# Five of six column blocks of a gMLP's input projection as matmuls of 64 rows, two token tiles at a time

## The chip, the cores and the metric

The kernel runs on one core of a Trainium2 chip. The metric is the device time of one execution in microseconds (us), given as the median of several runs. The engines are TensorE (PE, with weight loads, PEld, shown apart), VectorE (DVE), ScalarE (ACT), GpSimd (POOL) and SyncE (SP), which here only issues DMA transfers.

## The reference, cut to what matters

```python
def reference(A_x, A_wqkv, A_wo, B_x, B_w_in, B_w_sp, B_b_sp, B_w_out):
    # S = 2048 tokens, D = 576, 32 heads of 18, window 256, F = 4608, Fh = 2304
    xn = _layernorm(x)
    s = _A_ref(xn, A_wqkv, A_wo)          # causal sliding-window attention, then @ wo
    ...
    z = _gelu(xn @ w_in)                  # in _B_ref
    z1, z2 = z[..., :Fh], _layernorm(z[..., Fh:])
    g = einsum("ts,bsf->btf", w_sp, z2) + b_sp
    g = _silu((z1 * g) @ w_out)
    return x + s * g
```

The part that is changed is the right half of `xn @ w_in`, here called z2: 2048 tokens by 576 features times 576 by 2304.

## The kernel before, in words

All products are to be exact to about fp32. TensorE works on fp32r operands, so each factor is split into a high and a low part (`split`, L112 to L114: ACT copies the high part, DVE subtracts it from the source for the low one), and a product is three passes: high by high, low by high, high by low. The transposed, normalised input stays on chip as nine planes of 128 partitions: planes 0 to 3 hold the high parts of 512 features, planes 4 to 7 their low parts, and plane 8 the tail, 64 features with the high part on partitions 0 to 63 and the low part on 64 to 127. `norm_chunk` makes them for 512 tokens at a time: for the tail ACT copies the transposed tile (in which the 64 features stand twice), and DVE subtracts that copy from the source on the upper partitions (L290). The weights' tail stands twice as well, so two passes do for the tail, and `passes` (L221) yields 4 × 3 + 2 = 14 passes for an output tile.

The stages follow each other: input and norm with the q and k projections (`qk_chunk`), v, **z2**, attention with the z1 projection interleaved, wo, the products with w_sp, and the output. In a trace of before, z2 lies from 200.42 to about 441 us.

z2 is computed in six column blocks (`pc`) of 384 columns (ZW), each over 16 token tiles (`s`) of 128 tokens. For a tile, 14 matmuls (L720) accumulate in a PSUM bank `mm` (pool `mmp`, two buffers): the plane's 128 by 128 piece is the loaded operand, the weight's 128 by 384 piece the moving one. Then ACT evicts it with the gelu into half of a tile `zt` (L730; four buffers), DVE takes the statistics for z2's layernorm (L731), and after every second tile ACT issues the store of `zt` into `z2_d` in DRAM (L733). Three other strands run in the same loop:

- **Weights.** `load_z2(pc + 1)` (L673) fetches the next block's weights in three pieces of 128 columns: SP loads a piece into `z1wh` or `z1wl`, used here as raw buffers (L683), and ACT and DVE split it into `z2wh` and `z2wl`. It is a generator that is advanced at every second token tile. Block 0's weights were put in two of the attention's slots, `att0` and `att1`, and these are set to zeros and ones again (`clear`, L352 to L355, one by DVE and one by POOL) at the head of block 1.
- **Combinations of w_sp.** `sp_combos` (L642), a generator too, prepares sums of quadrants of w_sp for a later stage with fewer products: 16 steps, each with four SP loads (L651), four additions or subtractions on POOL (L661 to L665) and four SP stores into `sc_d` (L668), with two buffers of each kind. It is advanced at every second token tile.
- **Attention's operands.** From block 3 on, SP loads of the first heads (`pair_jobs`, L381); in block 5 the first row maxima (`row_max`, L428) lie between the passes.

The order on the engines: the gate, as this section is called, is within `order` (L671), which keeps the written order on PE, POOL and DVE (`ENGINES = {ET.PE, ET.Pool, ET.DVE}`, L55). The instructions of ACT and SP, and so all DMA issues, are put in order by a planner that simulates a timeline with its own costs (`schedule_with_timeline_sim=True`). From the attention on ACT and SP keep the written order too (L777). A tile's writers and readers wait for each other by semaphores that the framework inserts; completions of the DMAs are counted on eight semaphores that SP's and ACT's transfers share.

Of the kernel before, what the change touches and what calls it, by code (L numbers as in the profile page):

```python
# [9 lines left out]
F32 = mybir.dt.float32  # L10
F32R = mybir.dt.float32r
AF = mybir.ActivationFunctionType
ALU = mybir.AluOpType
PSUM = bass.MemoryType.PSUM
DRAM = bass.MemoryType.DRAM

P = 128
# [7 lines left out]
NS = S // P  # L25
# [3 lines left out]
ZW = 384  # L29
# [28 lines left out]
def f32(ap):  # L58
    return ap.bitcast(F32)
# [3 lines left out]
def kernel(  # L63
# [13 lines left out]
    act, dve, pool, pe, sp = nc.scalar, nc.vector, nc.gpsimd, nc.tensor, nc.sync  # L77

    def open_pool(stack, name, bufs=1, **kw):
        return stack.enter_context(tc.tile_pool(name=name, bufs=bufs, reuse_waits="tile", **kw))  # L80
# [9 lines left out]
    z2_d = dram.tile([S, FH], F32, name="z2_d")  # L90
# [14 lines left out]
    st2 = const.tile([P, NS, 6, 6], F32, name="st2")  # L105
# [21 lines left out]
    zt = []  # L127
# [57 lines left out]
    def plane(n, cs):  # L185

        i = 2 * n + cs.start // HS
        c0 = i % 3 * HS + cs.start % HS
        return xt6[i // 3][:, c0:c0 + cs.stop - cs.start]
# [6 lines left out]
    raws, halves, wpools = {}, {}, []  # L196
# [20 lines left out]
    with ExitStack() as early:  # L217
# [16 lines left out]
        with ExitStack() as ph:  # L234
# [23 lines left out]
            def norm_chunk(c):  # L258
                st = pA.tile([P, 4, 2, 6], F32, name="st")
                mv = pA.tile([P, 4, 2], F32, name="mv")  # L260
                sd = pA.tile([P, 4], F32, name="sd")
                rs = pA.tile([P, 4], F32, name="rs")
                tm = pA.tile([P, 4], F32, name="tm")
                step = 2 if c == 0 else 4
                for i0 in range(0, 4, step):
                    b = slice(i0, i0 + step)
                    for i in range(i0, i0 + step):
                        xr = xs[4 * c + i]
                        for j in range(2):
                            dve.bn_stats(st[:, i, j, :], xr[:, j * 288:(j + 1) * 288])  # L270
                        dve.bn_aggr(mv[:, i, :], st[:, i].rearrange("p a b -> p (a b)"))
                    rsqrt_of(rs[:, b], mv[:, b, 1], sd[:, b], tm[:, b])
                    for i in range(i0, i0 + step):
                        xr = xs[4 * c + i]
                        dve.tensor_scalar(xr[:, :D], xr[:, :D], mv[:, i, 0:1], rs[:, i:i + 1], ALU.subtract, ALU.mult)
                        pool.tensor_copy(xr[:, D:640], xr[:, 512:576])
                cs = slice(c * 512, (c + 1) * 512)
                for k in range(5):
                    t = tp.tile([P, 512], F32, name="tpt")
                    for i in range(4):  # L280
                        pe.transpose(t[:, i * P:(i + 1) * P], xs[4 * c + i][:, k * P:(k + 1) * P], ident)  # L281
                    if c == 0 and k < 2:
                        for i in range(3 + 3 * k):
                            pe.transpose(warm_up[:, k, i % 4 * P:(i % 4 + 1) * P], xs[3][:, :P], ident)
                    if k < 4:
                        split(plane(k, cs), plane(4 + k, cs), t)
                    else:
                        tail = plane(8, cs)
                        act.activation(tail, t, AF.Copy)
                        dve.tensor_tensor(tail[64:128], t[64:128], f32(tail[64:128]), ALU.subtract)  # L290

            def qk_chunk(c):
                cs = slice(c * 512, (c + 1) * 512)
# [54 lines left out]
        with ExitStack() as ph:  # L348
# [323 lines left out]
            with ExitStack() as gate:  # L672
                def load_z2(pc):  # L673
                    if pc:
                        wh, wl = (gz.tile([P, 5, ZW], F32R, name=n) for n in ("z2wh", "z2wl"))
                    else:
                        wh, wl = (slots[i][:, :5 * ZW].rearrange("p (k n) -> p k n", k=5) for i in range(2))

                    def pieces():
                        for c in range(3):  # L680
                            cs = slice(c * P, (c + 1) * P)
                            raw = f32(zw.tile([P, 5, P], F32R, name=("z1wh", "z1wl")[c % 2]))
                            sp.dma_start(raw, w_z2[:, :, pc * ZW + c * P:pc * ZW + (c + 1) * P])  # L683
                            yield
                            split(wh[:, :, cs], wl[:, :, cs], raw)
                            yield

                    return wh, wl, pieces()

                nxt = load_z2(0)  # L690
                for _ in nxt[2]:
                    pass
                for _ in vm:
                    pass
                values.close()
                gz = open_pool(gate, "gz", bufs=2)
                ahead = iter(())
                combos = sp_combos(gate)
                pairs = []
                for pc in range(6):  # L700
                    zc = slice(pc * ZW, (pc + 1) * ZW)
                    wh, wl, _ = nxt
                    if pc + 1 < 6:
                        nxt = load_z2(pc + 1)
                    if pc == 1:
                        clear(0)
                        clear(1)
                    if pc == 3:
                        pairs = [job for p in range(2) for job in [pair_jobs(p)] for _ in range(8)]
                    if pc == 5:  # L710
                        pairs = [job for job in [pair_jobs(2)] for _ in range(8)]
                        ahead = row_max(0)
                    for s in range(NS):
                        ss = slice(s * P, (s + 1) * P)
                        if pairs:
                            next(pairs.pop(0))
                        ps = mmp.tile([P, 512], F32, name="mm")
                        pl = list(passes(wh, wl, ss))
                        for n, (wt, r) in enumerate(pl):
                            pe.matmul(ps[:, :ZW], r, wt, start=n == 0, stop=n == len(pl) - 1)  # L720
                            if n in (3, 7, 11):
                                next(ahead, None)
                        if (pc * NS + s) % 2 == 1:
                            next(combos, None)
                        if pc + 1 < 6 and s % 2 == 0:
                            next(nxt[2], None)
                        if s % 2 == 0:
                            zz = gz.tile([P, 2 * ZW], F32, name="zt", bufs=4)
                        zv = zz[:, s % 2 * ZW:s % 2 * ZW + ZW]
                        act.activation(zv, ps[:, :ZW], AF.Gelu_apprx_tanh)  # L730
                        dve.bn_stats(st2[:, s, pc, :], zv)  # L731
                        if s % 2 == 1:
                            act.dma_start(z2_d[(s - 1) * P:(s + 1) * P, zc].rearrange("(a p) c -> p a c", p=P),  # L733
                                          zz.rearrange("p (a c) -> p a c", a=2))
                        if pc == 5 and s == 6:
                            z1_first.append(load_z1(0))
                        if pc == 5 and s == 12:
                            while z1_first[0][2]:
                                z1_first[0][2].pop(0)()
                        if pc == 5:  # L740
                            spend(0 if s < 12 else 1000)
                            dve.bn_aggr(mv2[:, s, :], st2[:, s].rearrange("p a b -> p (a b)"))
                for _ in ahead:
                    pass
                for _ in combos:
                    pass
                sd2 = gz.tile([P, NS], F32, name="sd2", bufs=1)
                tm2 = gz.tile([P, NS], F32, name="tm2", bufs=1)
                rsqrt_of(rstd2, mv2[:, :, 1], sd2, tm2)
                dve.tensor_tensor(nmr2, mv2[:, :, 0], rstd2, ALU.mult)  # L750
                dve.tensor_scalar(nmr2, nmr2, -1.0, None, ALU.mult)
# [23 lines left out]
            with ExitStack() as heads:  # L775
# [21 lines left out]
                for u in range(NU):  # L797
# [22 lines left out]
                    while due[0] or due[1] or filled < quota:  # L820
# [9 lines left out]
                        _, kind, n = due[pick[1]].pop(0)  # L830
# [6 lines left out]
                        s, j = items[n]  # L837
# [42 lines left out]
        with ExitStack() as ph:  # L880
# [39 lines left out]
            for n in range(NS):  # L920
                t, c = divmod(n, 2)
# [37 lines left out]
    with ExitStack() as ph:  # L959
# [180 lines left out]
        for m, (g, n, s) in enumerate(order_sp):  # L1140
            k = PRODUCTS[n][1]
# [3 lines left out]
            wh, wl, zh, zl = halves.pop(m)  # L1145
            for j in range(6):
                c, p = divmod(j, 3)
                cs, ps = slice(c * 512, c * 512 + 512), slice(p * P, p * P + P)
                for i, (z, w) in enumerate(((zh, wh), (zh, wl), (zl, wh))):
                    pe.matmul(acc[j], z[:, ps], w[:, cs], start=s == i == 0 and n in OPENS,  # L1150
                              stop=s == 7 and i == 2, skip_group_check=True)
# [34 lines left out]
    with ExitStack() as ph:  # L1186
# [25 lines left out]
        nxt = load_y(CH[0])  # L1212
# [92 lines left out]
```

## Time and profile before

| | us |
|---|---|
| median of the runs shown (3) | 1955.36 |
| lowest, highest | 1953.27, 1958.51 |
| span of the profiled execution | 1949.2 |
| PE busy in it | 1931.0 (99%) |
| DVE, ACT, POOL busy | 1050.1, 897.2, 283.5 |

| stretch of the profiled execution | from, to (us) |
|---|---|
| input, norm, q, k and v | 0 to 200.4 |
| z2, blocks 0 to 4 | 200.42 to 397.35 |
| z2, block 5, with the first row maxima | 397.35 to about 441 |

The span is that of the engines' instructions in one execution taken with the profiler; it stands a few us under the times of the runs. Busy time on PE is modelled from its instructions' starts, so a busy PE need not be PE at its best rate. The view by windows gives, for a stretch, the busy time and the number of instructions of each engine, the granted TensorE clock as a share of full speed, the busy share of the DMA engines, and what they moved.

### The profile page before, as it was taken

What the parts mean: (1) busy time and instruction counts of PE and PEld (TensorE: products, weight loads), DVE (VectorE), ACT (ScalarE), POOL (GpSimd) and SP (SyncE); (2) the same over time, 40 slices, a digit from 0 to 9 for tenths busy, and PEclk for the clock granted to TensorE, in tenths of its full rate; (3) what the DMA queues carried; (4) which work ended last, traced back from release to release, by engine and by line L of the source; (5) the groups of instructions that cost most, each with busy time, mean ns of one, the idle gap of its engine ahead of it and who ended that gap; (6) DMA issues with size and microseconds to landing.
All of it is one profiled execution on the core that took longest, in us unless ns stands there. A gap on an engine that the chain in (4) does not pass through costs nothing.

```text
span 1949.2 us, 30859 instructions
## 1 busy us (share of the span) xinstructions
PE 1931.0 (99%) x11159; PEld 1656.4 (85%) x11159; DVE 1050.1 (54%) x2294; ACT 897.2 (46%) x1674; POOL 283.5 (15%) x362
## 2 busy tenths in 40 slices
PE   8999999999999999999999999999999999999999
PEld 7889999997777777777698888888888888899998
DVE  5511233366666666665226787757876567663222
ACT  4222322215555556566557675555554534442111
POOL 5001366103222222323200000000000000000000
PEclk9999999999999999999999999999999999999999
DMA  8655799424554556564567777776677555875441
GB/s 266 175 149 157 256 352 349 168 80 137 143 160 135 164 142 160 138 149 127 179 226 253 251 234 249 230 234 214 200 245 240 185 174 186 266 235 160 140 143 58
DMA packets 221513, 375.60 MB, mean 193 GB/s; under 512 B 43312, under 2 KB 118448, under 8 KB 221232
## 3 DMA queue, kind: packets, MB, share of 16 engines
q1 hardware_dynamic: 206000, 349.66, 57.9%
q10 hardware_dynamic: 15360, 23.97, 3.3%
q8 instruction: 88, 1.44, 0.3%
q14 instruction: 65, 0.53, 0.1%
HBM read 260.45 MB, written 112.83 MB: 192 GB/s over the span
## 4 chain that ended last, share of the span: by engine, by line
PE 91%; DMA 3%; DVE 2%; issue 2%; ACT 1%; POOL 1%; SPq 0%; ACTq 0%; DVEq 0%; POOLq 0%
PE acc L1150 32%; PE mm L484 12%; PE po L1243 12%; PE mm L720 9%; PE mm L312 6%; PE sp L428 5%; PE tps L554 5%; PE ops L578 4%; PE vps L504 3%; PE wops L910 3%; DMA a<-in_w_sp_dram 1%; DVE spl L114 1%; DMA zr<-z_d 1%; DMA sc_d<-a 0%; PE tpt L281 0%
## 5 line engine op out<-in xcount | busy, mean ns | idle before, releaser
L1150 PE MATMUL acc<-spl,zh 128*128 128x512 f32 x1008 | 392.6, 389 | 1.1 <-DVE spl L114 0.8
L1150 PE MATMUL acc<-sph,zl 128*128 128x512 f32 x1008 | 392.2, 389 | 0.0
L1150 PE MATMUL acc<-sph,zh 128*128 128x512 f32 x1008 | 392.2, 389 | 0.0
L432 DVE CUSTOM_DVE_ANT_0 junk<-sp,band 128x384 bf16<-128x384 f32 (+1 forms) x512 | 269.6, 538 | 160.4 <-PE sp L428 153.0
L558 ACT ACTIVATE pt<-tps 128x384 f32<-128x384 f32 (+2 forms) x576 | 243.7, 437 | 178.5 <-PE tps L554 168.8
L484 PE MATMUL mm<-b,z1wh 128*128 128x512 f32 x648 | 230.3, 395 | 0.0
L1150 PEld LDWEIGHTS acc<-spl,zh 128*128 128x128 f32 x1008 | 189.2, 188 | 41.7 <-DVE spl L114 2.8
L1150 PEld LDWEIGHTS acc<-sph,zh 128*128 128x128 f32 x1008 | 189.2, 188 | 39.4
L1150 PEld LDWEIGHTS acc<-sph,zl 128*128 128x128 f32 x1008 | 189.2, 188 | 39.1
L114 DVE TENSOR_TENSOR spl<-spr,sph 128x1024 fp32r<-128x1024 f32 x168 | 205.2, 1221 | 30.7 <-ACT sph L113 28.4
L113 ACT ACTIVATE zh<-b 128x384 fp32r<-128x384 f32 x168 | 87.5, 521 | 230.4 <-PE acc L1150 230.3
L720 PE MATMUL mm<-z2wh,b 128*128 128x384 f32 x720 | 191.4, 335 | 1.8 <-ACT zt L730 1.8
L554 PE MATMUL tps<-att 128*128 128x384 f32 (+1 forms) x576 | 184.3, 326 | 0.8 <-ACT pt L558 0.7
L428 PE MATMUL sp<-att 128*128 128x384 f32 (+1 forms) x512 | 177.1, 350 | 1.1 <-DVE mx L432 0.8
L113 ACT ACTIVATE sph<-spr 128x1024 fp32r<-128x1024 f32 x168 | 175.9, 1047 | 1.6 <-DMA spr<-sc_d 1.4
L114 DVE TENSOR_TENSOR zl<-b,zh 128x384 fp32r<-128x384 f32 x168 | 92.9, 553 | 149.7 <-ACT zh L113 144.3
L1243 PE MATMUL po<-b,yh 128*128 128x288 f32 x840 | 147.1, 295 | 0.5 <-ACT gs L1230 0.5
L731 DVE BATCH_NORM_STATS2 st<-zt 128x6 f32<-128x384 f32 x96 | 53.5, 559 | 167.7 <-ACT zt L730 167.7
L484 PE MATMUL mm<-b,z1wl 128*128 128x512 f32 x360 | 142.0, 395 | 0.0
L428 PEld LDWEIGHTS sp<-att 128*128 128x128 f32 x512 | 95.3, 187 | 51.0 <-issue 25.7
L720 PE MATMUL mm<-z2wl,b 128*128 128x384 f32 x400 | 133.7, 334 | 0.0
L720 PEld LDWEIGHTS mm<-z2wh,b 128*128 128x128 f32 x720 | 130.4, 188 | 3.0 <-ACT zt L730 3.0
(187 smaller groups left out, 2872.7 us busy)
## 6 DMA issues: line engine op xcount, KB each, us to landing
spr<-sc_d SPq DMA_DIRECT2D x96, 512.0 KB
spr<-in_w_sp_dram SPq DMA_DIRECT2D x72, 512.0 KB
zr<-z_d SPq DMA_DIRECT2D x144, 192.0 KB
st_d<-qkhl SPq DMA_DIRECT2D x72, 256.0 KB
z_d<-zt ACTq DMA_DIRECT2D x48, 384.0 KB
z_d<-z1o SPq DMA_DIRECT2D x72, 256.0 KB
z1t<-z_d SPq DMA_DIRECT2D x72, 256.0 KB
y_d<-z1t SPq DMA_DIRECT2D x72, 256.0 KB
```

The source lines that it names most:

```text
L113: act.activation(hi, src, AF.Copy)
L114: dve.tensor_tensor(lo, src, f32(hi), ALU.subtract)
L312: pe.matmul(ps, w, r, start=n == 0, stop=n == len(pl) - 1)
L428: pe.matmul(ps[:, :w], q_of(u, j)[:, i * P:(i + 1) * P], k_of(u, j)[:, k0:k0 + w], start=True, stop=True)
L432: dve.tensor_tensor_reduce(out=junk[:, :w], in0=ps[:, :w], in1=band[:, m0:m0 + w], scale=1.0, scalar=-3.0e38, op0=ALU.add, op1=ALU.max, ac ...
L484: pe.matmul(ps, w, r, start=n == 0, stop=n == len(pl) - 1)
L554: pe.matmul(ps[:, :m * P], k_of(u, j)[:, (kb - base) * P:(kb - base + 1) * P], q_of(u, j)[:, (a - lo) * P:(a - lo + m) * P], start=True, s ...
L558: act.activation(pt[:, j, d0:d0 + n * P], ps[:, (qa - a) * P:(qa - a + n) * P], AF.Exp, scale=scale)
L578: pe.matmul(o_ps[c][32 * j:32 * j + 32, (lo - 4 * c) * P:(hi - 4 * c + 1) * P], vgs[u][:, kb - k0, j * VW:j * VW + 32], pt[:, j, (lo - kb) ...
L720: pe.matmul(ps[:, :ZW], r, wt, start=n == 0, stop=n == len(pl) - 1)
L1150: pe.matmul(acc[j], z[:, ps], w[:, cs], start=s == i == 0 and n in OPENS, stop=s == 7 and i == 2, skip_group_check=True)
L1243: pe.matmul(po[i][:, a, :288], y if ahead else y[:, i * P:(i + 1) * P], w[a], start=f == 0 and m == 0, stop=f == NF - 1 and m == 2)
```

## The change

In blocks 0 to 4 each pass over 128 partitions becomes two matmuls of 64 partitions, a **lower** one (partitions 0 to 63) and an **upper** one (64 to 127), both into the same PSUM tile. The tile is called `zmm`, from a new pool `zps` of three buffers; block 5 keeps the passes of 128 and `mm`. `z2_halves` makes the two lists. The tail takes three half matmuls instead of two full passes: high by high, low by high, and high by low; low by low is no longer computed. The third one goes to the lower half for tiles whose tail has its high part below, and to the upper half for the others. For that `norm_chunk` now stores the tail of every second 256 tokens with the parts exchanged, by two subtractions (lines 290 and 291 of the changed kernel) on 64 partitions and 256 columns each in place of one. So a tile has 14 lower and 13 upper halves or the reverse, and the tiles are taken in the order 0, 2, 1, 3 of each four, so that these kinds alternate.

The loop over a tile emits its lower halves (line 757 there), and behind each of them one upper half of an earlier tile (`z2_upper`, line 732 of the changed kernel), if there is one in the list `upper`. For the first two tiles of block 0 this begins only with the seventh lower half (`LAG = 6`), so that the upper halves keep that distance from then on. Behind the lower halves of a tile DVE copies two of its columns into `between` (line 761 there), a small tile that nobody reads; in the framework's order the copy reads the bank after the lower halves, and the upper halves write it after the copy. When a tile's last upper half is emitted, `z2_evict` does what the loop did before: gelu (line 724 there), statistics (725), and the store (728) once both tiles of a `zt` are there. At the end of block 4 the upper halves that are left are emitted, and block 5 runs as before. The weights, the combinations and the attention's loads are advanced at the same tiles as before, and the clears of `att0` and `att1` are written at the head of block 1 as before; the upper halves left from block 0's last tiles come behind them.

In the built program PE's instructions are the same as before in kind and order, other than the 2160 halves in place of 1120 passes. Lines of the changed kernel are one higher than before from L292 on, and 58 higher from L772 on.

```diff
@@ -287,7 +287,8 @@
                     else:
                         tail = plane(8, cs)
                         act.activation(tail, t, AF.Copy)
-                        dve.tensor_tensor(tail[64:128], t[64:128], f32(tail[64:128]), ALU.subtract)
+                        for r, a in ((slice(64, 128), slice(0, 256)), (slice(0, 64), slice(256, 512))):
+                            dve.tensor_tensor(tail[r, a], t[r, a], f32(tail[r, a]), ALU.subtract)
 
             def qk_chunk(c):
                 cs = slice(c * 512, (c + 1) * 512)
@@ -697,6 +698,42 @@
                 ahead = iter(())
                 combos = sp_combos(gate)
                 pairs = []
+                zps = open_pool(gate, "zps", bufs=3, space=PSUM)
+                zts, open_, upper = {}, [], []
+                LAG = 6
+
+                def z2_halves(wh, wl, s, ps):
+                    ss = slice(s * P, (s + 1) * P)
+                    odd = s // 2 % 2
+                    halves = []
+                    for up, r in enumerate((slice(0, 64), slice(64, 128))):
+                        ms = [m for k in range(4) for m in ((plane(k, ss)[r], wh[r, k]), (plane(k, ss)[r], wl[r, k]),
+                                                            (plane(4 + k, ss)[r], wh[r, k]))]
+                        ms.append((plane(8, ss)[r], wh[r, 4]))
+                        if up == odd:
+                            ms.append((plane(8, ss)[r], wl[r, 4]))
+                        halves.append([partial(pe.matmul, ps[:, :ZW], x_, w_, start=not up and n == 0,
+                                               stop=n == len(ms) - 1, skip_group_check=True) for n, (x_, w_) in enumerate(ms)])
+                    return halves
+
+                def z2_evict(pc, s, ps):
+                    if s // 2 not in zts:
+                        zts[s // 2] = gz.tile([P, 2 * ZW], F32, name="zt", bufs=4)
+                    zz = zts[s // 2]
+                    zv = zz[:, s % 2 * ZW:s % 2 * ZW + ZW]
+                    act.activation(zv, ps[:, :ZW], AF.Gelu_apprx_tanh)
+                    dve.bn_stats(st2[:, s, pc, :], zv)
+                    if s % 2 == 1:
+                        zz = zts.pop(s // 2)
+                        act.dma_start(z2_d[(s - 1) * P:(s + 1) * P, pc * ZW:(pc + 1) * ZW].rearrange(
+                            "(a p) c -> p a c", p=P), zz.rearrange("p (a c) -> p a c", a=2))
+
+                def z2_upper():
+                    upper.pop(0)()
+                    open_[0][1] -= 1
+                    if not open_[0][1]:
+                        z2_evict(*open_.pop(0)[0])
+
                 for pc in range(6):
                     zc = slice(pc * ZW, (pc + 1) * ZW)
                     wh, wl, _ = nxt
@@ -710,7 +747,28 @@
                     if pc == 5:
                         pairs = [job for job in [pair_jobs(2)] for _ in range(8)]
                         ahead = row_max(0)
-                    for s in range(NS):
+                    for i in range(NS if pc < 5 else 0):
+                        s = i // 4 * 4 + (0, 2, 1, 3)[i % 4]
+                        if pairs:
+                            next(pairs.pop(0))
+                        ps = zps.tile([P, 512], F32, name="zmm")
+                        lo, up = z2_halves(wh, wl, s, ps)
+                        for n, m in enumerate(lo):
+                            m()
+                            if upper and (pc or i > 1 or n >= LAG):
+                                z2_upper()
+                        between = gz.tile([P, 2], F32, name="between")
+                        dve.tensor_copy(between, ps[:, 0:2])
+                        upper += up
+                        open_.append([(pc, s, ps), len(up)])
+                        if i % 2 == 1:
+                            next(combos, None)
+                        if i % 2 == 0:
+                            next(nxt[2], None)
+                    if pc == 4:
+                        while upper:
+                            z2_upper()
+                    for s in range(NS if pc == 5 else 0):
                         ss = slice(s * P, (s + 1) * P)
                         if pairs:
                             next(pairs.pop(0))
```

## The prediction

> **What bounds the kernel now.** I read the page's busy shares and its chain first, then the stretches of the z2 stage by window, then the timeline of single engines there.
>
> ```profile
> span 1949.2 us, 30859 instructions
> PE 1931.0 (99%) x11159; PEld 1656.4 (85%) x11159; DVE 1050.1 (54%) x2294; ACT 897.2 (46%) x1674; POOL 283.5 (15%) x362
> PE 91%; DMA 3%; DVE 2%; issue 2%; ACT 1%; POOL 1%; SPq 0%; ACTq 0%; DVEq 0%; POOLq 0%
> 275.00:311.00 36.00, 36.00 (x209) 35.83 (x208) 10.99 (x18) 9.26 (x18) 22.41 (x18) 1.00 1.02 362
> 311.00:347.00 36.00, 36.00 (x209) 35.82 (x208) 11.44 (x19) 9.26 (x18) 21.84 (x17) 1.00 0.94 342
> ```
>
> TensorE sets the end nearly everywhere: it is busy for 99% of the span and holds 91% of the chain. The last two lines are two stretches of the z2 stage (columns: length, PE, weight loads, DVE, ACT, POOL, clock, DMA share, GB/s). PE is full in them, but so are the DMA engines, at 362 GB/s and a share of 1.02. Most of those bytes are the w_sp combinations, which only use this stage as cover: z2 does not need them. The timeline gives PE's pace:
>
> ```profile
> 200.42 38.99 PE L720 MATMUL mm<-att,b 128*128 128x384 f32 x224
> 239.25 0.51 PE L720 MATMUL mm<-z2wh,b 128*128 128x384 f32 x2
> 397.35 0.51 PE L720 MATMUL mm<-z2wh,b 128*128 128x384 f32 x2
> ```
>
> Block 0 takes 239.25 − 200.42 = 38.83 us, 173.3 ns for each of its 224 passes. Block 5, which the change leaves as it is, starts at 397.35. I work out where it starts afterwards; all that follows it has the same instructions and shifts with it.
>
> **The matmuls.** Before, a token tile takes 14 passes, 1120 over five blocks. After, the lower halves number 14 and 13 in turn, 1080 in all, and an upper half of the tile before goes beside each. Upper halves lag by six slots and a tile, so 20 of them are left over at the end and run alone. That makes 1100 slots, 20 fewer: −3.5 us at 173.3 ns, if a pair costs what a full pass costs. No row shows halves of rows side by side. The nearest shows four column tiles:
>
> ```profile
> 457.67 1.50 PE L578 MATMUL ops<-pt,vg 128*32 128x384 f32 x16
> L578 PE MATMUL ops<-pt,vg 128*32 128x384 f32 x512 | 47.9, 492 | 0.0
> 10.09 0.93 PE L281 MATMUL tpt<-ident,xr 128*128 128x128 f32 x7
> L281 PE MATMUL tpt<-ident,xr 128*128 128x128 f32 x80 | 11.2, 273 | 0.0
> 199.09 0.69 PE L504 MATMUL vps<-whv,b 128*128 128x288 f32 x4
> L504 PE MATMUL vps<-whv,b 128*128 128x288 f32 x288 | 53.0, 294 | 0.0
> L720 PEld LDWEIGHTS mm<-z2wh,b 128*128 128x128 f32 x720 | 130.4, 188 | 3.0 <-ACT zt L730 3.0
> ```
>
> Sixteen matmuls of 492 ns each begin within 1.50 − 0.49 us, 67 ns apart on the mean, each with a load of its own: disjoint tiles run together, loads included. Halves of rows share no partition either, so I take 173 ns for a pair. Lower bound: four matmuls of 288 columns start every (0.69 − 0.29)/3 = 132 ns, so 96 columns cost 41 ns and 384 cost 165; the remaining 8 ns could vanish beside the other half. Upper bound: the two loads of a pair share one path; load and transpose of 128 columns follow each other every (0.93 − 0.27)/6 = 110 ns, so a pair would take 220.
>
> The Trainium skill ("TensorE: Matmul & The Clock Gate", Measured speedup vs the span model) gives four row tiles 3.07 times the speed of one after another; as an estimate by that rate a slot is 173/0.77 = 226 ns, and the sum below would be some 37 us higher. Its rule under The mechanism, that a weight load overlaps a running matmul only in another row group, would make pairing hide loads that are paid for today. The trace disagrees with it: loads of 188 ns disappear in intervals of 173 ns, all in the same rows.
>
> **The small additions.** 80 copies of two columns (between) go to DVE. Nearest rows, from both sides:
>
> ```profile
> L432 DVE DVE_READ_ACCUMULATOR2_ANT mx<- 128x1 f32 x32 | 2.7, 83 | 0.0
> L742 DVE BATCH_NORM_AGGREGATE mv<-st 128x2 f32<-128x36 f32 x15 | 4.8, 317 | 0.5
> L731 DVE BATCH_NORM_STATS2 st<-zt 128x6 f32<-128x384 f32 x95 | 53.0, 559 | 166.2 <-ACT zt L730 166.2
> 239.47 1.81 POOL L354 MEMSET att<- 128x2048 f32 x1 [16.92 <-PE mm L720]
> 241.22 1.17 POOL L355 MEMSET att<- 128x1280 f32 x1
> ```
>
> That is 7 to 25 us on an engine busy for 11 of 36 us: work beside PE. But the copy is a wait too. A tile's first upper half needs it six slots (1.0 us) after its last lower half, and everything on PE is queued behind that half. A copy that stands behind one statistic of 0.56 us makes it; one behind a late weight split does not, and I count that with the transfers below. The tail's subtraction in two instructions instead of one lies in the start and beside other work: nothing. The clears of the two slots are queued ahead of the last 20 upper halves of block 0, which so read cleared weights and wait for a memset of 1.8 us; before, no matmul waited for it.
>
> **What decides: the order of the transfers.** PE, DVE and POOL keep the written order. ACT and SP are ordered by the planner, which must take the 2160 half matmuls as one after another, for in the built program the combinations' transfers now stand far ahead of z2's steps. The transfers of SP and ACT share eight completion semaphores. So a z2 store on ACT waits for an SP transfer that was placed before it, and the next evictions queue behind the store. Counting the steps of each semaphore in the two built programs gives what the store after the n-th eviction waits for (16 steps of combinations, 0 to 15):
>
> ```
> after eviction   before                changed
> 4                load of step 1        load of step 3
> 20               store of step 2       load of step 10
> 24               store of step 4       load of step 15
> 28               store of step 5       store of step 14
> 52               load of step 12       (all steps are past)
> ```
>
> SP also carries block 3's third weight piece behind all 64 combination stores (before: between steps 6 and 7), and ACT splits it ahead of eviction 32. So the 16 steps must be through when about a third of the 80 tiles is, where before they were spread over all of z2. The trace shows that such a wait reaches PE, and what the steps need:
>
> ```profile
> 269.59 0.37 ACTq L733 DMA_DIRECT2D z_d<-zt  x1
> 270.08 0.87 ACT L730 ACTIVATE zt<-mm 128x384 f32<-128x384 f32 x2 [5.28 <-PE mm L720]
> 270.62 0.62 PE L720 MATMUL mm<-z2wh,b 128*128 128x384 f32 x2 [1.02 <-ACT zt L730]
> L665 POOL TENSOR_TENSOR a<-a,a 128x512 f32<-128x512 f32 x16 | 22.4, 1400 | 3.5 <-DMA a<-in_w_sp_dram 1.3 <-POOL a L664 1.1 <-DMA z_d<-zt 0.2
> L662 POOL TENSOR_TENSOR a<-a,a 128x512 f32<-128x512 f32 x16 | 21.2, 1327 | 8.6 <-DMA sc_d<-a 2.9 <-DMA a<-in_w_sp_dram 2.8 <-DVE st L731 1.2
> L664 POOL TENSOR_TENSOR a<-a,a 128x512 f32<-128x512 f32 x16 | 21.0, 1314 | 1.2
> L661 POOL TENSOR_TENSOR a<-a,a 128x512 f32<-128x512 f32 x16 | 20.7, 1291 | 42.8 <-DMA a<-in_w_sp_dram 31.9 <-issue 5.8 <-DMA sc_d<-a 5.1
> 280.31 1.29 POOL L661 TENSOR_TENSOR a<-a,a 128x512 f32<-128x512 f32 x1 [3.35 <-DMA a<-in_w_sp_dram]
> 321.54 1.28 POOL L661 TENSOR_TENSOR a<-a,a 128x512 f32<-128x512 f32 x1 [1.92 <-DMA sc_d<-a]
> 356.90 1.29 POOL L665 TENSOR_TENSOR a<-a,a 128x512 f32<-128x512 f32 x1
> a<-in_w_sp_dram SPq DMA_DIRECT2D x64, 256.0 KB
> sc_d<-a SPq DMA_DIRECT2D x64, 256.0 KB
> z_d<-zt ACTq DMA_DIRECT2D x31, 384.0 KB
> z1wh<-in_w_z_dram SPq DMA_DIRECT2D x8, 320.0 KB
> att<-st_d SPq DMA_DIRECT2D x8, 144.0 KB
> 220.17 0.49 SPq L651 DMA_DIRECT2D a<-in_w_sp_dram  x1
> 216.10 5.01 DMA a<-in_w_sp_dram
> 280.49 0.74 ACT L113 ACTIVATE z2wh<-z1wh 128x640 fp32r<-128x640 f32 x1 [1.76 <-PE mm L720]
> 282.39 0.47 ACT L730 ACTIVATE zt<-mm 128x384 f32<-128x384 f32 x1
> ```
>
> In the first three lines ACT stands before a late store, two evictions follow it at once, and PE stops for 1.02 us. The four L66x groups make POOL's own pace (22.4 + 21.2 + 21.0 + 20.7)/16 = 5.33 us a step; before, with the DMA engines full, five steps took (321.54 − 280.31)/5 = 8.2 each.
>
> **The sum.** (a) Step 3's first load goes out at 220.17 and takes 5 us to land: 225.2. Eviction 5 stands behind it, and tile 8, which needs that bank (there are three), would have begun at 200.42 + 7 × 13.5 × 0.1733 = 216.8; with the eviction PE stops 9 us. (b) Block 0 ends at 200.42 + 16 × 2.34 + 9 = 247. POOL has done two and a half steps by then, as before, and stands at its clear, whose 1.81 + 1.17 us let it go on at 250. (c) Eviction 28 needs 12.25 more steps: 12.25 × 8 × 256 KB = 25.7 MB, and beside them about 1.8 MB of att, six z2 stores (2.4 MB) and three weight pieces (1.0 MB), 30.9 MB. At 362 GB/s that is 85 us (bounds 65 at POOL's 5.33, 100 at 8.2). With 5 us to land: 340. (d) PE then stands before tile 31. Fifty tiles of 13.5 slots, 2.34 us each, are 117 us, the 20 leftover uppers 3.5. Three times ACT has three splits ahead of one eviction, 282.39 − 280.49 = 1.9 us in the last two lines; a bank that is held 34 slots and used again after 40.5 leaves little of it covered: 3 × 1.6 = 4.8. Block 5 starts at 465 against 397.35, +68, with bounds of +48 and +83 from (c). The −3.5 and the clear lie inside this. The span is 4 to 9 us under the three times shown, and what lies around it stays; so +68 goes onto the median, 1955.4: **2023 us**.
>
> **Rivals.** (1) Pairs overlap only in part, up to 220 ns: (50 × 13.5 + 20) slots × 47 ns, up to +33 on top, 2056; for it, that no row shows row tiles, against it, the column tiles. 17%. By the figure of the Trainium skill above this would be the case. (2) Pairs do not overlap: 2160 × 173.3 ns = 374 us instead of 194, the planner's order fits and nothing waits: +180, 2135. 7%. (3) The other side: the transfers do not hold z2, since each shared semaphore is passed in time. Then 1100 slots give −3.5, 1952, and at 165 ns −13, 1943. It decides by whether step 14 is stored when eviction 28 falls due, at 200.4 + 30 × 2.34 = 271; POOL alone needs until 250 + 65 = 315. 5%. My forecast has 71%.
>
> **The numbers.** The range goes from the POOL bound (2003) to 2071, the upper bound of the transfers with pairs that overlap in part on top (83 + 33); left out are rivals 2 and 3 and some tails, under 2 in 10. About 0.3% (5.9 us) is what a measurement of this kernel tells from no change; rival 3 is split 3 faster to 2 same, everything else is slower.
>
> **What would show it.** Right: POOL's last combination near 345 instead of 356.90; PE idle some 70 us between 215 and 345, ended by evictions (zt) that stand behind z_d stores or weight splits; half matmuls of one row group 173 ns apart; block 5 near 465, then the same distances as before. Wrong: PE without gaps from block 0 to block 5, with starts 87 ns apart (rival 3) or 173 (rival 2); or gaps ended by DVE alone, which would put the cost on the copies.

## The result and the profile after

The changed kernel takes 2029.53 us (median of 4 runs, 2028.14 to 2031.11) against 1955.01 for the kernel before: **slower by 3.8%**, ratio 1.0378 with a 95% interval of 1.0363 to 1.0393. The forecast was 2023, with a range of 2003 to 2071. The profiled execution's span is 2027.1 us, 77.9 more than before.

The page after, the same lines as were shown of before, and two stretches of the view by windows (columns as before):

```profile
span 2027.1 us, 33119 instructions
PE 1947.5 (96%) x12199; PEld 1668.2 (82%) x12199; DVE 1061.8 (52%) x2378; ACT 898.1 (44%) x1674; POOL 280.8 (14%) x362
PE 88%; DMA 6%; DVE 2%; ACT 1%; POOL 1%; issue 1%; SPq 1%; ACTq 0%; POOLq 0%; DVEq 0%
275.00:311.00 36.00, 16.80 (x126) 16.06 (x124) 3.57 (x10) 1.97 (x4) 25.62 (x21) 0.64 1.00 348
311.00:347.00 36.00, 15.38 (x128) 14.74 (x126) 4.94 (x10) 2.46 (x5) 27.25 (x22) 0.67 0.95 342
347.00:397.00 50.00, 48.93 (x564) 48.61 (x562) 16.69 (x45) 12.37 (x25) 0.00 (x0) 1.00 0.34 114
```

PE's busy time grew by only 16.5 us, so most of the loss is idle time, and DMA's share of the chain doubled. In the stretches 275 to 311 and 311 to 347 PE works for less than half of the time, while the DMA engines are full and POOL is at its combinations. From 347 on POOL has nothing left, and PE is nearly full with 564 halves in 48.9 us. The view of what PE waited for in z2 (columns: total us, times, longest), and ACT's timeline at the last large stalls:

```profile
PE zmm L757 <- ACT zt L724: 61.2, 10, 16.8
PE zmm L732 <- POOL att L355: 1.4, 1, 1.4
PE zmm L732 <- DVE att L355: 0.4, 1, 0.4
270.10 0.37 ACTq L728 DMA_DIRECT2D z_d<-zt  x1
270.58 0.49 ACT L724 ACTIVATE zt<-zmm 128x384 f32<-128x384 f32 x1 [11.67 <-DMA a<-in_w_sp_dram]
295.37 0.39 ACTq L728 DMA_DIRECT2D z_d<-zt  x1
295.85 0.49 ACT L724 ACTIVATE zt<-zmm 128x384 f32<-128x384 f32 x1 [17.93 <-DMA sc_d<-a]
330.78 0.43 ACTq L728 DMA_DIRECT2D z_d<-zt  x1
331.31 0.49 ACT L724 ACTIVATE zt<-zmm 128x384 f32<-128x384 f32 x1 [19.39 <-DMA a<-in_w_sp_dram]
338.81 0.37 ACTq L728 DMA_DIRECT2D z_d<-zt  x1
339.30 0.49 ACT L724 ACTIVATE zt<-zmm 128x384 f32<-128x384 f32 x1 [7.50 <-DMA a<-in_w_sp_dram]
```

Each time a store of z2 goes out only when a load or a store of the combinations has landed, and the eviction right behind it lets PE go on. An eviction needs nothing of those transfers; it stands behind the store on ACT's queue.

Block 5 starts at 474.40 (L778) against 397.35, 77.05 later. The parts of this: z2 starts 1.5 later (201.88); 20 slots fewer, −3.5; waits 63.0 after against 1.8 before, +61.2; a slow clock behind the waits, some +14 (below); the rest, some 4, is mostly the ends of the waits, since the view counts idle time from a matmul's modelled end. How the clock shows in PE's timeline:

```profile
222.04 0.68 PE L757 MATMUL zmm<-att,b 64*128 64x384 f32 x1 [8.07 <-ACT zt L724]
222.53 0.52 PE L757 MATMUL zmm<-att,b 64*128 64x384 f32 x1
222.84 0.52 PE L757 MATMUL zmm<-att,b 64*128 64x384 f32 x1
225.72 0.39 PE L757 MATMUL zmm<-att,b 64*128 64x384 f32 x1
225.95 0.33 PE L757 MATMUL zmm<-att,b 64*128 64x384 f32 x1
226.12 0.33 PE L757 MATMUL zmm<-att,b 64*128 64x384 f32 x1
```

After the stall of 8.07 us lower halves start 0.32 us apart, at a granted clock of 0.50, and 3.7 us later 0.17 apart. Over blocks 0 to 4, 99 starts of lower halves come more than 0.2 us after the one before without an idle stretch between, the first one behind each stall not counted; they add 14 us over 0.173 each. The Trainium skill ("TensorE: Matmul & The Clock Gate", What's actually happening) states this: an idle window halves the clock, and some 3.4 us of work bring it back. The trace agrees at this stall, though in e8 below the clock behaved otherwise; the prediction had left it out.

### The profile page after: what moved, and what is told of

Read it like the earlier page. It is cut to its first block, busy times and chain, and to the rows that moved or that the text cites. A ratio compares the mean times of both kernels' runs of the same rounds, so it can differ in the third digit from the quotient of the medians.

```text
span 2027.1 us, 33119 instructions
## 1 busy us (share of the span) xinstructions
PE 1947.5 (96%) x12199; PEld 1668.2 (82%) x12199; DVE 1061.8 (52%) x2378; ACT 898.1 (44%) x1674; POOL 280.8 (14%) x362
## 4 chain that ended last, share of the span: by engine, by line
PE 88%; DMA 6%; DVE 2%; ACT 1%; POOL 1%; issue 1%; SPq 1%; ACTq 0%; POOLq 0%; DVEq 0%
PE acc L1208 31%; PE po L1301 11%; PE mm L485 11%; PE zmm L757 7%; PE mm L313 5%; PE sp L429 5%; PE tps L555 5%; PE ops L579 4%; PE wops L968 3%; PE vps L505 3%; PE mm L778 2%; DMA a<-in_w_sp_dram 2%; DMA sc_d<-a 1%; DMA zr<-z_d 1%; DMA z_d<-zt 1%
## 5 line engine op out<-in xcount | busy, mean ns | idle before, releaser
L757 PE MATMUL zmm<-z2wh,b 64*128 64x384 f32 x576 | 157.6, 353 | 52.2 <-ACT zt L724 52.1
L757 PEld LDWEIGHTS zmm<-z2wh,b 64*128 64x128 f32 x576 | 111.7, 199 | 55.2 <-ACT zt L724 55.2
L732 PE MATMUL zmm<-z2wh,b 64*128 64x384 f32 x576 | 154.4, 349 | 0.0
L725 DVE BATCH_NORM_STATS2 st<-zt 128x6 f32<-128x384 f32 x80 | 44.8, 561 | 177.8 <-ACT zt L724 177.8
```

Of the source, the lines that this page charges most:

```text
L732: upper.pop(0)()
L757: m()
```

## The experiments

Two theories. **The order**: the planner puts the combinations' transfers far ahead, and z2's stores wait for them through the shared semaphores. **The pairs**: the halves, the copies between them or the bytes themselves cost the time. In this table the lengths are read from the traces: from the first matmul of z2 to the first of block 5. Each ratio is to runs of the kernel before that were taken beside that kernel's own, so it is not the quotient of two rows.

| kernel | median us | ratio to before, 95% | z2 starts | blocks 0 to 4 |
|---|---|---|---|---|
| before | 1955.01 | | 200.42 | 196.9 |
| changed | 2029.53 | 1.0378 (1.0363 to 1.0393) | 201.88 | 272.5 |
| e1 paced | 1975.99 | 1.0105 (1.0088 to 1.0122) | 201.40 | 213.9 |
| e2 written order | 2033.32 | 1.0404 (1.0389 to 1.0420) | 209.66 | 268.5 |
| e3 before, written order | 1973.66 | 1.0101 (1.0085 to 1.0116) | 209.69 | 209.8 |
| e4 mended | 1967.61 | 1.0068 (1.0053 to 1.0083) | 208.23 | 202.6 |
| e5 POOL stores | 1972.69 | 1.0092 (1.0073 to 1.0111) | 201.09 | 216.8 |
| e6 before, POOL stores | 1953.70 | 0.9999 (0.9990 to 1.0008) | 200.92 | 194.5 |
| e7 clean | 1948.52 | 0.9969 (0.9957 to 0.9981) | 201.49 | 190.5 |
| e8 blocks | 2272.45 | one run | 200.84 | 514.7 |
| e9 blocks, clean | 2073.87 | one run | 201.14 | 315.2 |
| e10 clears on DVE | 2025.43 | one run | 201.87 | 268.9 |

**e1, the combinations paced by z2.** The edit:

```diff
+ last_.append(st2[:, s, pc, 0:1])          # in z2_evict, behind the statistic
  if i % 2 == 1:
+     if last_:
+         pool.tensor_copy(gz.tile([P, 1], F32, name="pace"), last_[-1])
      next(combos, None)
```

> The changed kernel with one thing added: before each advance of the combinations in blocks 0 to 4 POOL copies one element of the latest z2 statistic (40 copies of one column), so that the combinations, and in the planner's order their transfers, cannot run ahead of z2's evictions. In the built program the store after eviction 28 then waits for a load of step 5 instead of a store of step 14, the one after eviction 20 for none past step 3. Theory (the planner's order, through the shared completion semaphores, holds the evictions): the 61 us of PE waiting for evictions and the slow-clock stretches behind them mostly go; what is left is the pairs' own 1100 slots x 0.1734 = 191 us, the clear and the splits, some 5 to 20 us of gaps: block 5 starts at 400 to 418 instead of 474.4, time 1957 to 1975. Rival 1 (the pairs, the copies into between, or the bytes themselves cost the time): the same bytes and the same halves stay, so 2015 to 2030.

1975.99, 1 us over the theory's range: the same halves, copies and bytes, and 54 of the 75 us are gone. The waits for evictions fall from 61.2 to 9.6 us; the clear is now a wait of 4.3, since POOL comes to it later:

```profile
PE zmm L757 <- ACT zt L724: 9.6, 6, 4.2
PE zmm L732 <- POOL att L355: 4.3, 1, 4.3
```

**e5, the stores of z2 from POOL; e6, the same in the kernel before.** One word in each (in e6 for block 5's stores too):

```diff
- act.dma_start(z2_d[...
+ pool.dma_start(z2_d[...
```

> The changed kernel with one word changed: the z2 stores of blocks 0 to 4 are issued by POOL instead of ACT. POOL's transfers are counted on semaphores of their own, so these stores wait for no transfer of the combinations, and no eviction on ACT stands behind a store. The combinations' transfers stay far ahead in SP's order, as in the changed kernel. Theory (stores that wait on a shared semaphore hold the evictions): the three large stalls between 262 and 340 (9.1 + 15.3 + 3.9 + 16.8 + 3.8 us) go; those at the splits and at the clear stay: block 5 at 405 to 420, time 1963 to 1978. Rival 1 (the early transfers themselves hold z2, by their bytes or by SP's order): 2015 to 2030. Rival 2 (the pairs cost it): 2015 to 2030.

> The kernel before with all its z2 stores issued by POOL instead of ACT: the counterpart of e5 with full passes. Its stores stalled PE for 1.8 us; with POOL's, 0 to 1.8 us less and nothing else: 1950 to 1956. If issuing from POOL costs time by itself (POOL's combinations or DVE slowed), 1960 or more.

e5 took 1972.69, as expected, with all halves in place, and PE's waits for evictions fell as in e1:

```profile
PE zmm L757 <- ACT zt L724: 13.2, 6, 5.9
```

So most of the time is lost where a store of z2 waits for a foreign transfer, with the evictions behind it. The traces carry the numbers of the semaphores, and they bear this out: in the changed kernel the combinations' loads and stores and z2's stores count on the same eight, and the five z2 stores that end the large stalls each wait, just ahead of their issue, on the very one that they are to count on; e5's stores on POOL count on eight others. But e5 is not a test of the semaphores alone. POOL's additions now queue behind its stores, which wait for evictions, and this paces the transfers as much as e1 does: the first load of step 8 leaves SP at 286.70 in the changed kernel, at 320.89 in e5 and at 321.50 in e1. What speaks against the transfers' bytes as the cause is the kernel before. There the same loads leave SP at nearly the same times as in the changed kernel (the first of step 3 at 220.17 against 221.45, of step 8 at 280.02 against 286.70, of step 15 at 341.79 against 332.11), and its PE is full beside them. So in the changed kernel the transfers are not early in time; they are ahead only of the z2 stores that wait for them.

e6 shows that the store on POOL by itself is worth nothing with full passes (ratio 0.9999). Its first five blocks of z2 take 194.5 us instead of 196.9, but that gain does not show in the times:

```profile
200.92:395.46 194.54, 194.54 (x1123) 194.01 (x1121) 72.00 (x96) 50.96 (x100) 102.32 (x93) 1.00 0.77 259
```

**e2 and e3, ACT and SP in the written order in the z2 section**, with halves and with full passes:

```diff
- order.enter_context(tc.manual_schedule(engines=ENGINES))
+ order.enter_context(tc.manual_schedule(engines=ENGINES | {ET.Activation, ET.SP}))
```

> The changed kernel with ACT and SP in the written order in the z2 section too; nothing else is changed. The order of the instructions on each engine is then mended, but the completion semaphores are still dealt out by the planner's clock: the store after eviction 28 waits for a store of step 6, after eviction 56 for a load of step 12. If the order on SP alone were the cause, the time would come back to 1955 to 1965. If the dealing out of the shared semaphores is the cause as well, stalls of 5 to 10 us spread over all five blocks instead of three large ones before 345, and only part comes back: block 5 at 440 to 468, time 1995 to 2023. If the pairs themselves cost the time: 2015 to 2030, with starts of one row group further apart than 173 ns.

> The kernel before with ACT and SP in the written order in the z2 section, full passes of 128 rows. It tells whether the written order by itself is worth or costs something. With full passes the planner's clock is right and the semaphores fit: block 5 within 3 us of 397.35, 1951 to 1958. If the written order itself stalled z2 (SP standing at stores behind POOL), it would be slower by 10 us or more, and e2 would say nothing about the pairs.

Both missed. e2 came out at 2033.32, no better than the changed kernel: the waits for evictions are 55.6 us, though spread, as expected, over all five blocks. e3 shows why this edit is no mending: with full passes it costs 20 us too. Its z2 starts 9.3 us later, since the section's order also holds the last part of v, and PE waits 12.1 us for evictions:

```profile
PE mm L720 <- ACT zt L730: 12.1, 7, 3.2
```

So the written order has prices of its own. Still, e2 says two things. Where nothing waits, its starts of one row group are 173 ns apart, so the pairs cost no more than full passes. And with the order on ACT and SP mended, ACT still waits for the combinations' transfers ahead of evictions, 61.7 us against 64.6 in the changed kernel, and PE for ACT:

```profile
ACT zt L724 <- DMA sc_d<-a: 36.3, 6, 15.5
ACT zt L724 <- DMA a<-in_w_sp_dram: 25.4, 3, 9.6
PE zmm L757 <- ACT zt L724: 55.6, 10, 12.9
```

So the order on the queues is not the whole of the tie. Why the same written order makes PE wait 55.6 us with halves and 12.1 with full passes is not shown; that the planner's clock deals out the semaphores is the expectation's reason, and no run tests it.

**e4, several stalls mended at once.** e1's edit, and:

```diff
+ order over ACT too (from the end of v on)
- act.dma_start(z2_d[...                 # z2's stores
+ sp.dma_start(z2_d[...
- zps bufs=3, zt bufs=4
+ zps bufs=4, zt bufs=5
- clear(0); clear(1)                     # at the head of block 1, DVE and POOL
+ both on POOL, at tiles 2 and 8 of block 2
```

> The changed kernel with what the trace blames taken away: POOL paced as in e1; ACT in the written order in the z2 section, so that the weight splits lie between evictions; the z2 stores issued by SP, so that no eviction queues behind a store, with five buffers of zt; four banks of zmm; both clears on POOL, at tiles 2 and 8 of block 2, behind block 0's last upper halves. Theory: PE runs through blocks 0 to 4 with under 4 us of gaps; 1100 slots x 0.1734 = 190.7 us against 196.9 before, block 5 3 to 6 us earlier than before relative to z2's start: 1949 to 1953, so the pairs are worth their 20 slots fewer plus what before stalled (1.8 us), and no more. If pairs cost more than a full pass beside transfers (say 180 ns), 1957 or more.

1967.61, 15 us over the upper end of what was expected. Half of the miss is the late start of z2 (208.23), as in e3. The other half is three waits and a slow clock behind two of them: stores on SP stand behind the combinations there, ACT waits for a free `zt` (up to 6.32 us), statistics and copies queue behind it on DVE, and PE waits for a copy, 6.9 us in all:

```profile
PE zmm L732 <- DVE between L761: 6.9, 3, 3.9
315.36 0.87 ACT L724 ACTIVATE zt<-zmm 128x384 f32<-128x384 f32 x2 [6.32 <-DMA z_d<-zt]
```

**e7, every stall taken away.** Against the changed kernel:

```diff
+ order.close()                           # behind the v stage
+ order.enter_context(tc.manual_schedule(engines=ENGINES | {ET.Activation}))
  gz = open_pool(gate, "gz", bufs=2)
- zps bufs=3, zt bufs=4
+ zps bufs=4, zt bufs=5
- act.dma_start(z2_d[...                 # blocks 0 to 4
+ pool.dma_start(z2_d[...
- if pc == 1:
-     clear(0)
-     clear(1)
+ if pc == 2 and i in (2, 8):
+     clear(i // 8, pool)
```

> The changed kernel with every stall that its trace shows taken away: z2 stores of blocks 0 to 4 on POOL, ACT in the written order from the start of z2 (not in the v stage, where e4 lost 8 us), four banks of zmm, five buffers of zt, both clears on POOL at tiles 2 and 8 of block 2. Theory: PE runs without gaps, 1100 slots x 0.1734 = 190.7 us from z2's start to block 5 against 196.9 before: 1946 to 1951, the whole worth of the pairs being 20 slots (3.5 us) and the 1.8 us of stalls and some slow clock that before had. If a pair costs more than a pass when it isn't held, 1955 or more.

1948.52, and the view by windows over blocks 0 to 4 (columns as before) has PE busy for all of them, at full clock:

```profile
201.49:392.00 190.51, 190.51 (x2160) 190.26 (x2160) 73.92 (x174) 49.53 (x95) 103.70 (x95) 1.00 0.79 263
```

1100 slots in 190.51 us are 173.2 ns a slot, the price of a full pass. This version is faster than the kernel before too, but only by 0.3% (ratio 0.9969, interval 0.9957 to 0.9981). With e6, whose stores are on POOL too and whose PE shows no gap either, the comparison is 190.5 against 194.5 us: by these two traces the pairs are worth 4.0 us, of which the 20 slots make 3.5.

**e8 and e9, halves in rows:** the upper halves of a tile in one row behind the next tile's lower halves, in the changed kernel and in e7.

```diff
  for n, m in enumerate(lo):
      m()
-     if upper and (pc or i > 1 or n >= LAG):
-         z2_upper()
+ while upper:                            # the number at this point
+     z2_upper()
```

> The changed kernel with the upper halves of a tile emitted in one row behind the lower halves of the next tile, instead of one behind each lower half: the same halves, banks, copies and transfers, but neighbours of the same row group. Theory (halves of disjoint rows run side by side, those of one group take 173 ns each): 2160 x 0.1734 = 374.5 us instead of 191 from z2's start to block 5. If, as the prediction's rival 2 had it, the planner's order fits such a z2, nothing waits: 2135. In the built program the store after eviction 27 still waits for a load of step 15, so some stalls between 290 and 360 may stay: up to 2165. If pairs did not overlap in the changed kernel either, the time would be that of the changed kernel, 2030.

> e7 with the halves in rows as in e8: a tile's upper halves in one row behind the next tile's lower ones. No transfer and no split holds z2 in e7, so this tells whether e8's clock of 0.50 came from its stalls or from the halves themselves. Theory A (a matmul that uses half of the rows, alone on the array, counts as half a load for the clock, so the granted clock falls to 0.5 some 50 us into z2 and stays there without any gap): about 0.24 us a half as in e8's last blocks, 2160 x 0.24 = 518 us, less at full clock in the first 50 us: z2's start to block 5 450 to 515 us, time 2205 to 2275. Theory B (the clock fell in e8 since PE stood still for 10 us and more, and the stalls kept it there): clock 1.00 throughout, 0.1734 us a half or a little less where rows of two groups meet, 340 to 375 us, time 2095 to 2135.

Both came out otherwise. The first of these two lines is of e8, the second of e9, from the view by windows:

```profile
406.00:506.00 100.00, 100.00 (x417) 99.76 (x417) 12.10 (x35) 7.59 (x16) 0.00 (x0) 0.50 0.12 42
406.00:506.00 100.00, 100.00 (x697) 99.96 (x697) 20.24 (x57) 15.46 (x31) 32.43 (x31) 1.00 0.45 152
```

In e9 100 us hold 697 halves, 143 ns each: less than 173, since some of the halves at a border between two rows run together, but far from the 87 ns of pairs. So interleaving is worth 315.2 − 190.5 = 125 us in a z2 that nothing holds. In e8 the same halves run at a granted clock of 0.50 and 240 ns each; the clock fell at 252.56, behind a wait of only 1.66 us, and stayed there until 720.19, 4.7 us into block 5 with its full passes, though PE shows no gap from 361 to 710. e9, with no gap before 510, stays at 1.00 until then. So the half-used rows alone do not lower the clock (theory A of e9 falls), but once lowered it did not come back on them. Why is open. Of the prediction's rival 2, that a z2 without overlap would fit the planner's order, e8 shows the contrary: ACT still waited for stores of the combinations,

```profile
ACT zt L724 <- DMA sc_d<-a: 25.8, 2, 17.9
```

and PE in the end for copies that queued on DVE behind the statistics of those evictions, 17.2 us.

**e10, both clears on DVE.**

```diff
- clear(0)
- clear(1)
+ clear(0, dve)
+ clear(1, dve)
```

> The changed kernel with both clears on DVE, so that POOL does not stand at its clear (28.4 us there, from 222 to 250.7) and goes on with the combinations. Nothing else is changed in the source; the planner's order is made anew, and the store after eviction 20 now waits for a store of the last but one step. The prediction's sum says that z2 goes on when the transfers are through and then needs its remaining tiles. The steps can now run without a pause from 208: 16 steps at 362 GB/s (33.6 MB and some 5 MB beside) are through near 310, and 58 tiles x 2.34 + 3.5 + about 4 us of gaps follow: block 5 at 445 to 465, time 2000 to 2020. If the transfers' end doesn't set it (the pairs, the copies): 2030 as before.

2025.43 in its one run, a gain of 4 instead of 10 to 30 us; blocks 0 to 4 are 3.6 us shorter. The transfers did end sooner, though 14 us after the 310 that was expected: the last large stall ends at 324.30 against 339.84. But in the new order, as expected, it is an earlier store that waits for them, and more of z2 is left (the counts of lower halves behind the last large stall: first the changed kernel, two groups, then e10):

```profile
L757 PE MATMUL zmm<-z2wh,b 64*128 64x384 f32 x477 | 123.6, 337 | 7.1 <-ACT zt L724 7.0
L757 PE MATMUL zmm<-z2wl,b 64*128 64x384 f32 x238 | 79.8, 335 | 0.0
L757 PE MATMUL zmm<-z2wh,b 64*128 64x384 f32 x522 | 135.1, 337 | 19.6 <-ACT zt L724 19.6
L757 PE MATMUL zmm<-z2wl,b 64*128 64x384 f32 x261 | 87.6, 336 | 0.0
```

715 lower halves are 53 tiles, 783 are 58: five tiles of 2.34 us take back 12 of the 15.5 us.

## Why the prediction was right, step by step

- **What decides** was named rightly: e1, e5 and e7 show that the halves are not what costs, and the traces show that the stores which wait on shared semaphores for the combinations' transfers are. What was only argued is that the planner's view of the halves as one after another made that order; no run tests the planner's costs.
- **The price of a pair**: 173 ns forecast, 173.2 measured in e7, with loads of 64 rows hidden. The bound of 220 ns, and the estimate of 226 ns from the Trainium skill ("TensorE: Matmul & The Clock Gate", Measured speedup vs the span model), are out for two row tiles of this size.
- **(a) The first stall**: 9 us forecast, 8.07 measured, but ended by another transfer than named and at another tile, so that the sizes agree is luck. It was eviction 3 that came late, not eviction 5, and PE stood from 213.97, not from 216.8. ACT stood before a split of block 2's weights, whose load SP had issued at 215.97 between the combinations:

```profile
215.97 0.56 SPq L684 DMA_DIRECT2D z1wh<-in_w_z_dram  x1
220.87 0.74 ACT L113 ACTIVATE z2wh<-z1wh 128x640 fp32r<-128x640 f32 x1 [10.01 <-DMA z1wh<-in_w_z_dram]
```

- **(b) and (c) The clear and the transfers**: POOL was to go on at 250; it stood before its clear until 250.67 and went on at 253.5. The last large stall was to end at 340 and ended at 339.84. That it fits so well is luck in part: the sum's own bounds were 320 and 355, and the transfer that ended it was another one (see d), a load of step 15, which SP issued side by side with the stores of step 14. POOL's last combination was expected near 345 and started at 343.38.

```profile
250.67 1.80 POOL L355 MEMSET att<- 128x2048 f32 x1 [28.40 <-PE zmm L732]
343.38 1.28 POOL L666 TENSOR_TENSOR a<-a,a 128x512 f32<-128x512 f32 x1
```

- **(d) What is left** was sized too small, and this is where the 9.4 us between 465 and 474.4 come from. It was not eviction 28, behind a store of step 14, that was freed last, but eviction 25, behind the store that waits for a load of step 15, as the prediction's own table has it; so 53 tiles were left, not 50 (+7 us). The splits cost three times 1.07, not 1.6 (−1.6). The half clock behind each stall was not in the sum at all; behind the last one, with the ends of the stalls, it is taken to make the remaining 4 us. In the time the miss is smaller, 6.5 us, by chance: the profiled execution of before was a short one, its span 4 to 9 us under the times shown, where that of the changed kernel lies 1.8 us under its own time.
- **The small additions**: the copies took 157 ns each on the mean, 12.6 us on DVE, beside other work; the clear cost PE 1.4 + 0.4 us where 1.8 was named. The tail's two subtractions are not seen: z2 starts 1.5 us later, of which 0.85 is a wait for v's eviction.
- **Rivals**: the other side (1943 to 1952, transfers that do not hold z2) is the kernel that e7 makes, 1948.52. It was rightly priced; the edits of e7 make it come true.

## What to carry to other kernels

Before weighing what matmuls cost, look at what a change does to an order that a planner makes from its own costs: here passes worth 4 us were saved, and some 75 us of waits and slow clock came with them. Queue entries that may wait for somebody else's transfer (stores that share a completion semaphore) should not stand ahead of what frees the bottleneck's buffers; moving 40 stores to another queue, which also paced the transfers, was worth 57 us. And in these runs halves of the array's rows paid only interleaved one by one: that makes a pair as cheap as one full pass, and no cheaper, so what is won is only the passes that are dropped.

## What the hardware showed that was not expected

- Two halves of rows from two tiles, interleaved, start 173.2 ns a pair, with the weight loads of both (183 ns each in e7) hidden.
- Halves emitted in rows of 13 or 14 overlap at the borders of the rows: 143 ns a half on the mean in e9 instead of 173.
- On halves in rows a granted clock of 0.50 came behind a wait of 1.66 us and stayed for over 300 us without a gap (e8), where the same halves without an earlier stall kept 1.00 (e9); pairs brought it back in 3.7 us, and block 5's full passes in 4.7. The cause is open.
